# Turning Y into the FFN's input on VectorE, in 16 transposes of 32 rows, instead of on TensorE, from chunk 2 on

## The chip, the cores and the metric

One core of one Trainium2 chip. The metric is the device time of one execution in microseconds (us), on the slowest core, which here is the only one. Medians are over runs of one set; the ratio is the mean time of one kernel's fast runs over that of the other's of the same rounds, so it is not quite the ratio of the medians.

## The reference, cut to what matters

```python
def _attn_ref(q, k, v, beta):              # B=4, H=8, S=768, D=48
    k_n = k / (np.linalg.norm(k, axis=-1, keepdims=True) + 1e-06)
    for t in range(S):
        y[:, :, t] = einsum('bhd,bhde->bhe', q[:, :, t], state)
        v_old = einsum('bhde,bhd->bhe', state, k_n[:, :, t])
        state = state + beta[t] * outer(k_n[:, :, t], v[:, :, t] - v_old)
    return y

x = y.transpose(0, 2, 1, 3).reshape(B * S, H * D)      # (3072, 384)
out = (silu(x @ w_gate) * (x @ w_val)) @ w_out         # d_ff = 1536
```

The kernel walks through the sequence in 12 chunks of 64 positions. A chunk's Y comes out with the token on the partition (128 rows: two batches of 64 positions) and 768 columns. The FFN's products contract over the 384 features, so the FFN needs them on the partition: x_ffn, 128 partitions by 3 parts by 256 tokens. Turning Y into x_ffn is what the change is about.

## The kernel before

While TensorE does the FFN of chunk c, the recurrence of chunk c+1 is done in steps between its products. The order on each engine is that of the program's text. One step of the recurrence ends in Y, the next one turns it:

```python
    # advance(c), its last two steps
        p_of_u()
        y = work.tile([128, NB, NJ, 2, D], FP32, name="y", tag="r", bufs=2)
        for bp in each:
            nc.scalar.copy(y[:, bp, :, 0], p_y[:, 0, bp])
            for b in range(2):
                nc.scalar.copy(y[half_of(b), bp, :, 1], p_y[half_of(1 - b), 1, bp])
        yield

        y_f = y.rearrange("p bp j par d -> p bp (j par d)")
        xts[c] = ffn_pool.tile([128, KT, TOK], FP32, name="x_ffn")
        p_f = ps_pair("p_f", "py")[:, :, 0 : KT * 128]
        ...
        for bp in range(NB):
            for t in range(KT):
                nc.tensor.transpose(p_f[:, t, bp], y_f[:, bp, at], ident)   # 6 products
        for bp in each:
            nc.scalar.copy(x_v[:, :, bp], p_f[:, :, bp])                    # the copy
        yield
```

VectorE's work between the FFN's products: h_f (gate times value), sums of h_f, the adds of the fast output, the steps of an inverse (two instructions each, tmp and zb, handed out by `fill`), and the turning of k and q in whole, into kt and qt, which TensorE needs for the products of k with k and of q with k ("Gram products" here, p_g). The traces count two instructions for each call of an FFN product, so six calls show as x12; the transposes of Y on TensorE count one.

```python
            nc.vector.transpose(xt, blocks...)       # kt and qt, 128x1024 each, in front of their Gram products
    ...
    def gate_val(c, f, fill, within=None):           # six times a chunk
        ... 6 products p_gate; sil on ScalarE; fill(2); 6 products p_val
        nc.vector.tensor_tensor(out=hs[c, f], in0=sil, in1=ps["p_val"], op=ALU.mult)
        ... sums_of_h
        fill(3)
```

And in the fast output VectorE's adds stand between products. `product(1, 1)` is called twice with one tile, and between the two calls `add` reads it:

```python
        product(1, 0, ...); add(o[1][:, right], o[0][:, right], p[1, 0])
        fill(2)
        point(c + 1)                                 # the next chunk's step: here Y is turned, for even chunks
        product(0, 0, ...); nc.scalar.copy(o[0][:, left], p[0, 0])
        for f in range(0, FH, 2):
            minus(h_of(c, f + FH, 0), h_of(c, f + FH, 0), s_of(2, f))      # three
        product(1, 1, lambda f: s_of(1, f), ...)
        add(o[1][:, right], o[1][:, right], p[1, 1])
        point(c + 1)                                 # kt and qt
        product(1, 0, ...); add(o[1][:, left], o[0][:, right], p[1, 0])
        product(1, 1, lambda f: h_of(c, f + FH, 0), quarter(1, 1))         # same tile as above
```

Of the kernel before, what the change touches and what calls it, by code (L numbers as in the profile page):

```python
# [16 lines left out]
R = 32  # L17
# [4 lines left out]
def kernel(  # L22
# [25 lines left out]
    nc = tc.nc  # L48
# [4 lines left out]
    NB = B // 2  # L53
    DM = H * D
    DFF = moe_w_gate.shape[1]
    KT = DM // 128
# [13 lines left out]
    def ps_pair(name, tag):  # L70

        return psum.tile([128, 2, 512], FP32, name=name, tag=tag, bufs=1)
# [17 lines left out]
    def slot(c):  # L90
        return c if c < AHEAD else (c - AHEAD) % (AHEAD - 1)

    def freed_by_k(c):

        return c - AHEAD if c < 2 * AHEAD - 1 else c - AHEAD + 1
# [21 lines left out]
    def load_k(c, dmas=(nc.sync,)):  # L117
        for n in range(2 * NB):
            bp, b = divmod(n, 2)
            dmas[n % len(dmas)].dma_start(  # L120
                out=knp[slot(c)][64 * b : 64 * b + 64, bp, :, 0:D],
                in_=halves(k, c, bp, b).rearrange("h p d -> p h d"),
            )
# [37 lines left out]
    def load_v(c):  # L161
        vin[c] = work.tile([128, 2, NB, NJ, D], FP32, name="vin", bufs=2)
        for bp in range(NB):
            for b in range(2):
                src = halves(v, c, bp, b).rearrange("(j par) p d -> par p j d", par=2)
                for par in range(2):
                    s = 64 * (b ^ par)
                    nc.sync.dma_start(out=vin[c][s : s + 64, par, bp], in_=src[par])
# [161 lines left out]
    kt, qt, a_sb, a_of, p_sb, xts = {}, {}, {}, {}, {}, {}  # L330
# [3 lines left out]
    def half_of(x):  # L334
        return slice(64 * x, 64 * x + 64)

    def every():
        for bp in range(NB):
            for j in range(NJ):
                for n, (par, b) in enumerate(ORDER):  # L340
                    yield bp, j, par, b, bp == 0 and j == 0
# [56 lines left out]
    def scale_v(c):  # L398
        r = vin[c].rearrange("p par bp j d -> p (par bp j) d")
        n = n_t[c // 2][:, c % 2, :, None].to_broadcast([128, HH, D])  # L400
        nc.vector.tensor_tensor(out=r, in0=r, in1=n, op=ALU.mult)
# [171 lines left out]
    def recur(p, m=D):  # L573
        p = p[:, :, 0 : NB * NJ * m]
        return p.rearrange("p x (bp j d) -> p x bp j d", bp=NB, j=NJ)
# [154 lines left out]
    def advance(c):  # L730

        kn = knp[slot(c)]
        zt = ztp[c // 2 % ZB][:, c % 2]
        zt = zt.rearrange("p (par bp j) i -> p par bp j i", par=2, bp=NB)
        if c > 0:
            scale_v(c)
        r = vin.pop(c)
        p_y = recur(ps_pair("p_y", "py"))
        if c > 0:
            p_r = recur(ps_pair("p_r", "px"))  # L740
            for bp, j, par, b, first in every():
                nc.tensor.matmul(  # L742
                    p_r[half_of(b ^ par), par, bp, j],
                    kt[c][half_of(par), bp, j, b],
                    state[half_of(par), b, bp, j],
                    start=first,
                    stop=True,
                    skip_group_check=True,
                )
            for bp, j, par, b, first in every():  # L750
                nc.tensor.matmul(  # L751
                    p_y[half_of(b ^ par), par, bp, j],
                    qt[c][half_of(par), bp, j, b],
                    state[half_of(par), b, bp, j],
                    start=first,
                    stop=False,
                    skip_group_check=True,
                )
            nc.vector.tensor_tensor(out=r, in0=r, in1=p_r, op=ALU.subtract)  # L759
        yield  # L760
        p_u = recur(ps_pair("p_u", "px"))
        for bp, j, par, b, first in every():
            nc.tensor.matmul(  # L763
                p_u[half_of(b), par, bp, j],
                zt[half_of(b ^ par), par, bp, j],
                r[half_of(b ^ par), par, bp, j],
                start=first,
                stop=True,
                skip_group_check=True,
            )  # L770
        uu = work.tile([128, 2, NB, NJ, D], FP32, name="uu", tag="r", bufs=2)
        each = range(NB) if c == 0 else (slice(0, NB),)
        for bp in each:
            nc.scalar.copy(uu[:, :, bp], p_u[:, :, bp])
        if c + 2 < NCH:
            load_v(c + 2)
        yield
        pq = p_sb.pop(c)

        def p_of_u():  # L780
            for bp, j, par, b, first in every():
                nc.tensor.matmul(  # L782
                    p_y[half_of(b ^ par), par, bp, j],
                    pq[half_of(b), par, bp, j],
                    uu[half_of(b), par, bp, j],
                    start=(c == 0 and first),
                    stop=True,
                    skip_group_check=True,
                )

        def of_state():
            p_s = recur(ps_pair("p_s", "px"))
            for bp, j, par, b, first in every():
                nc.tensor.matmul(  # L794
                    p_s[half_of(par), b, bp, j],
                    kn[half_of(b), bp, 2 * j + par],
                    uu[half_of(b), par, bp, j],
                    start=first,
                    stop=True,
                    skip_group_check=True,  # L800
                )
            if c > 0:
                nc.vector.tensor_tensor(out=state, in0=state, in1=p_s, op=ALU.add)
            else:
                nc.scalar.copy(state, p_s)
            for later in range(AHEAD, NCH):
                if freed_by_k(later) == c:
                    load_k(later)

        if 0 < c < NCH - 1:  # L810
            of_state()
# [7 lines that stand above are left out]

        y_f = y.rearrange("p bp j par d -> p bp (j par d)")  # L820
        xts[c] = ffn_pool.tile([128, KT, TOK], FP32, name="x_ffn")
        p_f = ps_pair("p_f", "py")[:, :, 0 : KT * 128]
        p_f = p_f.rearrange("p bp (t n) -> p t bp n", t=KT)
        for bp in range(NB):
            for t in range(KT):
                at = slice(t * 128, (t + 1) * 128)
                nc.tensor.transpose(p_f[:, t, bp], y_f[:, bp, at], ident)
        x_v = xts[c].rearrange("p t (bp n) -> p t bp n", bp=NB)
        for bp in each:
            nc.scalar.copy(x_v[:, :, bp], p_f[:, :, bp])  # L830
        yield
        if c == 0:
            of_state()
            yield
# [256 lines left out]
    def point(c):  # L1091

        mine = c < NCH and steps("advance", c) < 4 and may_advance(c)
        if mine and steps("advance", c) > 0:
            step("advance", advance, c)
        elif not prep_step(c - 1) and mine:
            step("advance", advance, c)

    def finish(c):

        if c < NCH:
            while not may_advance(c):
                fill_some(1000)
                prep_step(c - 1)
            while steps("advance", c) < 4:
                step("advance", advance, c)
# [190 lines left out]
```

## Time and profile before

| | before |
|---|---|
| median of 4 runs | 738.61 us (738.02 to 739.34) |
| span of the profiled run | 737.5 us |
| TensorE, VectorE, ScalarE busy | 697.5, 473.1, 154.7 us |
| one set of six products, start to next start | 0.66 us |
| ScalarE's copy behind it | 0.80 us |
| places with a set from chunk 2 on | 10 |

The rows for the operations that go (60 of the 72 products and 10 of the 13 copies), as the view of one tile gives them (shortest, median and longest time of one in ns; first and last start in us). The 0.27 us of one product is not what it costs, as the products overlap:

```profile
L827 PE MATMUL p_f<-ident,y x72: 272/273/472, 61.6 to 664.4; 128*128 128x128 f32 x72
L830 ACT COPY x_ffn<-p_f x13: 480/799/801, 63.1 to 664.7; 128x768 f32<-128x768 f32 x11, 128x384 f32<-128x384 f32 x2
```

### The profile page before, as it was taken

Reading aid. Unit: us, or ns where it says so; the run is one execution under the profiler, and the core shown is the slowest. Engines: PE = TensorE matmul, PEld = TensorE weight load, DVE = VectorE, ACT = ScalarE, POOL = GpSimd, SP = SyncE. Lnnn points to the kernel's source line nnn. Section 1 sums busy time; section 2 is a strip of 40 time slices with the busy share of each in tenths; the row PEclk is TensorE's granted clock in tenths of the full one; section 3 lists DMA queues with packets and bytes.
Section 4 is the critical chain, followed back from the end, with each engine's and each line's share of the span. In section 5 each row is a group of like instructions: output and inputs, shape, how many; then the busy total and the mean of one; then the engine's idle time right before and its main releaser. Section 6 shows DMA issues by size and latency. Waiting matters only on the chain.

```text
span 737.5 us, 22478 instructions
## 1 busy us (share of the span) xinstructions
PE 697.5 (95%) x10132; PEld 604.7 (82%) x10132; DVE 473.1 (64%) x977; ACT 154.7 (21%) x287; POOL 66.9 (9%) x46
## 2 busy tenths in 40 slices
PE   4657899999999999999999999999999999999997
PEld 3546788866787788988988988988988988989987
DVE  5999988978498163678854678854578853313122
ACT  3455443302401112011012011012011012021010
POOL 7008100201200000030000030000030000000000
PEclk9556999999999999999999999999999999999999
DMA  6775444121231012331302231302210100100000
GB/s 141 164 227 166 124 108 129 36 41 24 56 45 24 22 24 45 43 67 15 53 3 45 36 70 20 53 3 39 46 29 12 32 3 3 23 3 0 22 1 21
DMA packets 130735, 37.18 MB, mean 50 GB/s; under 512 B 122864, under 2 KB 125936, under 8 KB 130640
## 3 DMA queue, kind: packets, MB, share of 16 engines
q1 hardware_dynamic: 127184, 34.01, 22.7%
q10 hardware_dynamic: 3072, 1.57, 1.0%
q8 instruction: 79, 1.29, 0.7%
q0 software_dynamic: 384, 0.17, 0.1%
q14 instruction: 16, 0.13, 0.1%
HBM read 31.01 MB, written 4.72 MB: 48 GB/s over the span
## 4 chain that ended last, share of the span: by engine, by line
PE 83%; DVE 14%; issue 1%; DMA 1%; ACT 0%; ACTq 0%; SPq 0%; DVEq 0%
PE p_gate L847 23%; PE p_val L847 23%; PE p_o L959 17%; PE p_o L876 6%; DVE tmp L510 3%; PE p_g L444 3%; DVE zb L516 3%; PE p_u L763 2%; PE p_r L742 1%; PE p_s L794 1%; PE p_y L782 1%; PE p_y L751 1%; DVE last_h L287 1%; PE p_t L432 1%; DVE h_f L862 1%
## 5 line engine op out<-in xcount | busy, mean ns | idle before, releaser
L847 PE MATMUL p_gate<-x_ffn,wg_sb 128*128 128x256 f32 x864 | 204.4, 387 | 1.5 <-ACT x_ffn L830 1.5
L847 PE MATMUL p_val<-x_ffn,wv_sb 128*128 128x256 f32 x864 | 198.5, 379 | 0.0
L847 PEld LDWEIGHTS p_val<-x_ffn,wv_sb 128*128 128x128 f32 x864 | 163.8, 190 | 22.3
L847 PEld LDWEIGHTS p_gate<-x_ffn,wg_sb 128*128 128x128 f32 x864 | 161.1, 191 | 24.2 <-ACT x_ffn L830 2.0
L862 DVE TENSOR_TENSOR h_f<-sil,p_val 128x512 f32<-128x512 f32 x71 | 48.6, 684 | 147.5 <-PE p_val L847 147.0
L856 ACT ACTIVATE sil<-p_gate 128x512 f32<-128x512 f32 x72 | 43.0, 598 | 276.9 <-PE p_gate L847 247.3
L655 POOL TENSOR_TENSOR n_b<-mb,half 128x32 f32<-128x32 f32 x5 | 43.0, 8607 | 408.6 <-DVE mb L480 368.2
L959 PE MATMUL p_o<-wo_sb,h_f 128*128 128x192 f32 x432 | 75.6, 328 | 0.1
L959 PEld LDWEIGHTS p_o<-wo_sb,h_f 128*128 128x128 f32 x432 | 70.3, 190 | 1.2 <-DVE o_sb L969 0.7
L510 DVE TENSOR_TENSOR tmp<-zb,mb 128x31 f32<-128x31 f32 (+15 forms) x186 | 63.3, 340 | 12.2 <-PE p_j L630 6.8
L516 DVE TENSOR_TENSOR zb<-zb,tmp 128x31 f32<-128x31 f32 (+15 forms) x186 | 63.7, 343 | 6.5 <-DVE tmp L510 0.2
L969 DVE TENSOR_TENSOR o_sb<-o_sb,p_o 128x192 f32<-128x192 f32 x45 | 15.8, 350 | 53.4 <-PE p_o L959 36.2
L876 PE MATMUL p_o<-wo_sb,h_f 128*128 128x384 f32 x136 | 45.7, 490 | 0.0
L876 PEld LDWEIGHTS p_o<-wo_sb,h_f 128*128 128x128 f32 x136 | 25.3, 190 | 16.5
L959 PE MATMUL p_o<-last_k,h_f 128*128 128x192 f32 x180 | 32.2, 326 | 0.0
L959 PEld LDWEIGHTS p_o<-last_k,h_f 128*128 128x128 f32 x180 | 29.7, 190 | 0.0
L917 DVE TENSOR_TENSOR h_f<-h_f,h_f 128x256 f32<-128x256 f32 x54 | 22.4, 424 | 8.0 <-PE p_o L959 7.1
L959 PE MATMUL p_o<-last_h,h_f 128*128 128x192 f32 x144 | 26.3, 326 | 0.0
L959 PEld LDWEIGHTS p_o<-last_h,h_f 128*128 128x128 f32 x144 | 23.9, 190 | 0.0
L254 ACT ACTIVATE last_h<-last_h,rebias 128x512 int32<-128x512 uint32 (+2 forms) x26 | 15.3, 616 | 30.5 <-DVE last_h L246 30.4
L763 PEld LDWEIGHTS p_u<-vin,zt 64*64 64x64 f32 x768 | 13.7, 141 | 6.9 <-issue 3.2
L763 PE MATMUL p_u<-vin,zt 64*64 64x48 f32 x768 | 15.7, 228 | 2.4 <-DVE vin L759 1.2
(180 smaller groups left out, 692.6 us busy)
## 6 DMA issues: line engine op xcount, KB each, us to landing
vin<-in_v_dram SPq DMA_DIRECT2D x96, 48.0 KB
kn<-in_k_dram SPq DMA_DIRECT2D x40, 96.0 KB
out_dram<-o_sb SPq DMA_DIRECT2D x36, 96.0 KB
zt<-in_moe_w_out_dram SPq DMA_DIRECT2D x6, 384.0 KB
staged<-in_moe_w_out_dram SPq DMA_DIRECT2D x6, 384.0 KB
qpad<-in_q_dram SPq DMA_DIRECT2D x36, 64.0 KB
wo_sb<-in_moe_w_gate_dram SPq DMA_DIRECT2D x4, 512.0 KB
wo_sb<-in_moe_w_val_dram SPq DMA_DIRECT2D x4, 512.0 KB
```

Of the source, the lines that this page charges most:

```text
L444: nc.tensor.matmul(p_v[par][half_of(b if of_q else b ^ par), bp, j], kt[c][half_of(par), bp, j, b], xt[half_of(par), bp, j, b],)
L510: nc.vector.tensor_tensor(out=t_v, in0=zb[:, 0 : j + 1, j : j + 1].to_broadcast([128, j + 1, m]), in1=mb[:, j : j + 1, j + 1 : R].to_broad ...
L516: nc.vector.tensor_tensor(out=zb[:, 0 : j + 1, j + 1 : R], in0=zb[:, 0 : j + 1, j + 1 : R], in1=t_v, op=ALU.add,)
L655: nc.gpsimd.tensor_tensor(out=n, in0=mb.rearrange("p j i -> p (j i)")[:, 0 : R * R : R + 1], in1=half, op=ALU.pow,)
L763: nc.tensor.matmul(p_u[half_of(b), par, bp, j], zt[half_of(b ^ par), par, bp, j], r[half_of(b ^ par), par, bp, j], start=first, stop=True, ...
L847: nc.tensor.matmul(ps[name][:, i], w_sb[:, t, (f + i) * 128 : (f + i + 1) * 128], xts[c][:, t], start=(t == 0), stop=(t == KT - 1),)
L856: nc.scalar.activation(sil, ps[name], ACTF.Silu)
L862: nc.vector.tensor_tensor(out=hs[c, f], in0=sil, in1=ps["p_val"], op=ALU.mult)
L876: nc.tensor.matmul(p_o, hs[c, f - f % 2][:, f % 2, bp * 128 : (bp + 1) * 128], wo_sb[:, f], start=(f == 0), stop=(f == FT - 1),)
L917: nc.vector.tensor_tensor(out=out, in0=a, in1=b, op=ALU.subtract)
L959: nc.tensor.matmul(p[x, part], a(f - f % 2)[:, f % 2], b(f), start=not begun and f == 0, stop=f == FH - 1, skip_group_check=True,)
L969: nc.vector.tensor_tensor(out=out, in0=a, in1=b, op=ALU.add)
```

## The change

TensorE is 95% busy and VectorE 64%, so the change takes the turning from TensorE (and ScalarE) and gives it to VectorE from chunk 2 on. The new transposes turn Y in blocks of 32x32. One instruction takes 32 rows of Y and the six blocks that belong to one quarter of x_ffn's partitions; four quarters of each make 16.

```diff
         xts[c] = ffn_pool.tile([128, KT, TOK], FP32, name="x_ffn")
+        if c > 1:
+            y_q = y_f.rearrange("p bp (t q d) -> p q t bp d", t=KT, q=4)
+            x_q = xts[c].rearrange("p t (bp q n) -> p q t bp n", bp=NB, q=4)
+            for of_x in range(4):
+                for of_y in range(4):
+                    nc.vector.transpose(
+                        x_q[R * of_x : R * of_x + R, of_y],
+                        y_q[R * of_y : R * of_y + R, of_x],
+                    )
+            yield
+            return
         p_f = ps_pair("p_f", "py")[:, :, 0 : KT * 128]
```

## The prediction

> **What bounds the kernel now.** I read the page first: busy shares, then the row of 40 slices, then the chain that ended last.
>
> ```profile
> span 737.5 us, 22478 instructions
> PE 697.5 (95%) x10132; PEld 604.7 (82%) x10132; DVE 473.1 (64%) x977; ACT 154.7 (21%) x287; POOL 66.9 (9%) x46
> PE   4657899999999999999999999999999999999997
> DVE  5999988978498163678854678854578853313122
> PE 83%; DVE 14%; issue 1%; DMA 1%; ACT 0%; ACTq 0%; SPq 0%; DVEq 0%
> ```
>
> From slice 6 on, TensorE is full and carries the chain; VectorE has 36% idle on average. That average invites the change: take work from the full engine, give it to the idle one. But VectorE's row swings between 3 and 8 with the period of two chunks, and the chain holds 14% DVE. The question is what VectorE does at the ten places where the new transposes stand. The program's order is fixed by hand, and comparing the instruction orders of the two kernels confirms it: nothing moves except that each set of six products leaves TensorE's order, each copy leaves ScalarE's, and each set of 16 transposes enters VectorE's.
>
> First, what TensorE gains. The timeline around one set (chunk 5's):
>
> ```profile
> 334.04 0.82 PE L827 MATMUL p_f<-ident,y 128*128 128x128 f32 x6
> 334.70 0.38 PE L847 MATMUL p_gate<-x_ffn,wg_sb 128*128 128x256 f32 x1
> ```
>
> Column one is the start, column two the time. The products are pipelined: the next product starts 0.66 us after the first of the six, not 0.82. So a set costs TensorE 0.66 us, and that is all that can be won in a place where TensorE is the bound.
>
> Second, where VectorE is the bound. The same chunk, ten microseconds later:
>
> ```profile
> 344.49 0.43 DVE L516 TENSOR_TENSOR zb<-zb,tmp 128x256 f32<-128x256 f32 x1
> 344.87 1.25 DVE L422 STREAM_TRANSPOSE kt<-qpad 128x1024 f32<-128x1024 f32 x1
> 346.04 1.20 DVE L422 STREAM_TRANSPOSE qt<-qpad 128x1024 f32<-128x1024 f32 x1
> 346.17 0.34 PE L444 MATMUL p_g<-kt 64*64 64x64 f32 x8 [0.94 <-DVE kt L422]
> ```
>
> TensorE already waits 0.94 us for VectorE's kt. The stretch from the h_f that starts at 334.31 (as TensorE ends p_val) to kt is full on VectorE; the stretches view gives it as follows (columns: stretch, length, busy of PE, PEld, DVE, ACT, POOL, clock):
>
> ```profile
> 334.30:344.90 10.60, 10.60 (x54) 9.33 (x51) 9.97 (x25) 1.99 (x3) 0.00 (x0) 1.00 0.00 0
> ```
>
> 9.97 of 10.60 us busy, the rest the 0.02 to 0.3 us between dependent instructions. There is no room in it, and the new transposes of chunk 5 stand in its middle, after the step that ends at 338.7. The timeline shows the same wait at 457.21 (0.95 us, chunk 7) and 568.36 (1.04 us, on qt, chunk 9).
>
> **What the Trainium skill says.** "VectorE: DVE Perf Modes", section "The three transpose paths": VectorE transposes only within 32x32 blocks, TensorE a full 128x128 into PSUM. Hence 16 instructions, one per pair of quarters. The trace has no 128x128 case on VectorE, but it has transposes of 32 rows into another quarter:
>
> ```profile
> 240.22 1.54 DVE L688 STREAM_TRANSPOSE z<-zt 32x256 f32<-32x256 f32 x4
> ```
>
> The same page, "Two Vector instructions with no wait between them": an instruction whose input starts in another quadrant than the last input is held until all earlier ones have finished. The trace agrees: these four start at 240.22, 240.59, 240.99, 241.36; 0.37 apart within a quadrant, 0.40 to 0.41 where the quadrant changes. All 16 new ones change the input quadrant each time.
>
> "TensorE: Matmul & The Clock Gate", section "Part 1: The HAM clock gate": after an idle window of about 3.4 us the array runs at half clock, until a busy window of that length. The trace agrees in its first 70 us (same columns; the clock is the number after POOL's):
>
> ```profile
> 29.80:33.20 3.40, 1.20 (x80) 1.06 (x72) 3.16 (x8) 1.07 (x2) 0.00 (x0) 1.00 0.52 94
> 33.20:63.90 30.70, 16.93 (x606) 14.23 (x597) 29.70 (x91) 19.23 (x51) 5.48 (x1) 0.50 0.65 174
> 63.90:67.30 3.40, 3.26 (x8) 2.64 (x9) 3.40 (x10) 1.43 (x3) 3.40 (x1) 0.50 0.81 201
> 67.30:70.70 3.40, 3.40 (x136) 2.87 (x135) 3.40 (x8) 1.82 (x3) 3.40 (x1) 1.00 0.54 176
> ```
>
> One window with 1.20 us of work of 3.40 dropped the clock to 0.5; it stayed there at half use and came back after one window with 3.26 of 3.40. So a wait of under 1 us costs itself, and a wait of 7 us costs something more.
>
> **The change part by part.** Removed: 10 sets of six products, 10 x 0.66 = 6.6 us of TensorE, and 10 ScalarE copies of 0.80 us (ScalarE is 21% busy: worth nothing by itself). Added: 160 transposes of 32x192. A column costs 1.07 ns (kt's 1024 columns take 1240 ns, z's 256 columns 415 ns in the mean). 64 columns fewer than z is 0.07 us less, so held ones follow each other at 0.405 - 0.07 = 0.335 us. A set takes T = 16 x 0.335 = 5.4 us, and 54 us for all ten; VectorE goes from 473 to about 527 us busy. I take the runs of 32 neighbouring columns at both ends, as z has them, for full speed. Now by place:
>
> Chunks 5, 7, 9 (transposes inside the full stretch): kt or qt comes T later, so the product that waits for it starts T later; 0.66 us saved on TensorE only lengthens the wait, to 0.94 + 0.66 + 5.4 = 7.0 us. Cost 5.4 each, 16.2 together. Nothing gives it back, as VectorE's next stretch starts again from a TensorE product.
>
> Chunk 2:
>
> ```profile
> 192.63 1.13 PE L847 MATMUL p_gate<-x_ffn,wg_sb 128*128 128x256 f32 x4 [0.52 <-ACT x_ffn L830]
> 193.04 0.28 DVE L516 TENSOR_TENSOR zb<-zb,tmp 128x112 f32<-128x112 f32 x1
> ```
>
> Here x_ffn is needed at once: TensorE waits for it 0.52 us even now. The new order puts the transposes behind the step that ends at 193.32, so x_ffn is whole at 193.35 + 5.4 = 198.75 and p_gate starts at about 198.8 instead of 192.63: cost 6.2.
>
> Chunks 4, 6, 8, 10 (transposes within the fast output of the chunk before):
>
> ```profile
> 297.15 0.35 DVE L969 TENSOR_TENSOR o_sb<-o_sb,p_o 128x192 f32<-128x192 f32 x1 [1.54 <-PE p_o L959]
> 298.46 0.43 DVE L917 TENSOR_TENSOR h_f<-h_f,h_f 128x256 f32<-128x256 f32 x1 [0.95 <-PE p_o L959]
> ```
>
> The transposes go between these two. They end at 297.5 + 5.4 = 302.9; the first h_f then ends at 303.35. TensorE needs it for the product that starts at 303.46 now and could start at 302.80 then. So the wait eats the 0.66 us, net about 0; kt and qt then follow at 305.4 and 306.6, which delays the qt product (306.48 now) by 0.2 in three of the four. Cost 0.6 together.
>
> Chunks 3 and 11: VectorE is idle behind the transposes (15.3 us before 257.07 in chunk 3; in chunk 11 no inverse is left to compute), and x_ffn is needed 10 and 24 us later. Gain 2 x 0.66 = 1.3.
>
> Sum: 6.2 + 16.2 + 0.6 - 1.3 = +21.7 us. To this comes the clock at the four long waits (chunks 2, 5, 7, 9: 6.7 to 7.0 us of idle TensorE, enough for a whole idle window). After each, TensorE runs at half clock for the rest of a window and then one whole one, 3.4 to 6.8 us, and loses half of that: an estimate of 2.2 us each from the lines above, 8.8 together. 738.3 + 21.7 + 8.8 = 768.8; I predict 768.
>
> **The rivals.** (a) TensorE stays the bound and all transposes hide: 738.3 - 6.6 and chunk 2's 0.5 to 1 us of waits gives 731, still within 2%. VectorE's 64% and the idle 36% speak for it; the full stretches before kt and the wait already there speak against it. (b) The waits come but the clock stays up: 760. The drop after a window with 1.20 us of work speaks against it. (c) The transposes run slower, as those with scattered columns do (32x1024 in 1941 to 2145 ns against 1216 for a plain one): a set would take about 8.6 us, each of eight places would pay 3.2 more, and the time would be near 794. The contiguous runs of 32 speak against it. (d) Transposes without holding, 0.30 apart, T = 4.8: eight places pay 0.6 less each, 764.
>
> **Range and chances.** T between 4.8 and 5.9 moves the sum by about 4 us each way, the clock's share lies between 4 and 14. I put the range at 756 to 781. 2% slower is 753, below even case (b). Faster by 2% is not reachable, as the whole TensorE cost removed is 0.9%. Chances: faster 0.01, within 2% 0.06, slower 0.93.
>
> **What would show it.** In the new profile: x_ffn transposes of 330 to 350 ns, sets of 5.2 to 5.6 us; TensorE waits of about 7 us for kt, kt and qt before the Gram products of three chunks and of over 6 us for x_ffn before chunk 2's first p_gate; a clock of 0.5 for a few us behind each; waits under 1 us in the four fast outputs; none in chunks 3 and 11. Wrong would be: sets much longer or shorter than 5.4, a TensorE row without holes, or a clock that stays at 1.0 behind them.

## The result, and the profile after

777.43 us (median of 4, 776.09 to 778.19) against 738.61 us: ratio 1.0523, 95% interval 1.0504 to 1.0542. The change makes the kernel 5% slower. The prediction was 768, with a range of 756 to 781.

The page of the changed kernel, its busy line, the rows by slices and the chain:

```profile
span 776.4 us, 22499 instructions
PE 702.4 (90%) x10072; PEld 608.2 (78%) x10072; DVE 530.5 (68%) x1137; ACT 146.5 (19%) x277; POOL 67.7 (9%) x46
PE   5657999998799999896999896999897899899997
DVE  5999989797498455879753969754778764626122
PEclk8657999999799999997999998999999899999999
PE 71%; DVE 24%; issue 2%; POOL 1%; DMA 1%; ACT 0%; SPq 0%; DVEq 0%
```

VectorE's share went up by only four points, and still 10% of the chain moved to it. TensorE's row, full from slice 6 on before, has holes, and the clock's row dips in four of those slices. TensorE is busy *longer* than before (702.4 against 697.5 us) although 60 products are gone: mostly work done at half clock (1.6 us of it lie in the first 150 us, where the two runs differ anyway).

The transposes themselves, in the view of the tile (times of one in ns):

```profile
L828 DVE STREAM_TRANSPOSE x_ffn<-y x160: 358/370/375, 193.2 to 711.3; 32x192 f32<-32x192 f32 x160
```

Chunk 5's turn in the timeline. Before, TensorE waited 0.94 us for this kt:

```profile
348.43 6.11 DVE L828 STREAM_TRANSPOSE x_ffn<-y 32x192 f32<-32x192 f32 x16
...
360.74 1.25 DVE L422 STREAM_TRANSPOSE kt<-qpad 128x1024 f32<-128x1024 f32 x1
...
362.04 1.98 PE L444 MATMUL p_g<-kt 64*64 64x64 f32 x64 [7.63 <-DVE kt L422]
```

The set takes 6.11 us, kt comes that much later, and the product behind kt waits 7.63 us. The product takes 1.98 us for what took 1.16. The stretches around it show why (columns: stretch, length, busy time of PE, PEld, DVE, ACT, POOL, clock):

```profile
356.60:366.90 10.30, 4.86 (x132) 4.74 (x133) 9.89 (x21) 0.60 (x1) 0.00 (x0) 0.50 0.20 27
366.90:370.30 3.40, 3.40 (x23) 3.40 (x22) 3.23 (x9) 0.32 (x1) 0.00 (x0) 1.00 0.66 85
```

The clock fell to 0.5 while TensorE waited and stayed there for almost 5 us after it had work again. In these traces it holds each value for 3.41 us or a whole multiple of that; one such stretch of 3.41 us is called a window below. Chunk 2, where x_ffn itself is late:

```profile
193.22 6.11 DVE L828 STREAM_TRANSPOSE x_ffn<-y 32x192 f32<-32x192 f32 x16
...
199.38 4.65 PE L859 MATMUL p_gate<-x_ffn,wg_sb 128*128 128x256 f32 x12 [7.30 <-DVE x_ffn L828]
```

And the fast output in front of chunk 4, where I had expected nothing worth naming:

```profile
305.64 6.11 DVE L828 STREAM_TRANSPOSE x_ffn<-y 32x192 f32<-32x192 f32 x16
...
311.78 1.09 DVE L929 TENSOR_TENSOR h_f<-h_f,h_f 128x256 f32<-128x256 f32 x3
312.80 0.35 DVE L981 TENSOR_TENSOR o_sb<-o_sb,p_o 128x192 f32<-128x192 f32 x1
...
313.20 2.22 PE L971 MATMUL p_o<-wo_sb,h_f 128*128 128x192 f32 x12 [2.01 <-DVE o_sb L981]
```

Where the 39 us went. I took the start of the first p_gate of every gate/value step in both traces and followed the shift between them; behind chunk 0, where it swings by up to 1.2 us and ends at -0.05, the shift changes only at the places of the change and just behind them. A long wait's own part is read at the start of the product that waits, the rest up to the next FFN step is put down to the clock.

| place | predicted | the wait, net | behind it, clock 0.5 | sum |
|---|---|---|---|---|
| chunk 2 | 6.2 | 6.80 | 1.79, and 0.34 at a Gram product for which VectorE is late | 8.93 |
| chunk 5 | 5.4 | 6.02 | 1.60 | 7.62 |
| chunk 7 | 5.4 | 6.02 | 1.18 | 7.20 |
| chunk 9 | 5.4 | 5.92 | 2.56 | 8.48 |
| chunks 4, 6, 8, 10 | 0.6 together | 1.63, 1.62, 1.62, 1.63 | 1.57 behind chunk 8's | 8.07 |
| chunks 3, 11 | -1.3 | -0.66, -0.65 | none | -1.31 |
| clock | 8.8 | | (8.70, in the rows above) | |
| all | 30.5 | | | 38.99 |

The spans differ by 776.4 - 737.5 = 38.9.

### The profile page after: what moved, and what is told of

Its sections match the earlier page's. It is cut to its first block, busy times and chain, and to the rows that moved or that the text cites. A ratio compares the mean times of both kernels' runs of the same rounds, so it can differ in the third digit from the quotient of the medians.

```text
span 776.4 us, 22499 instructions
## 1 busy us (share of the span) xinstructions
PE 702.4 (90%) x10072; PEld 608.2 (78%) x10072; DVE 530.5 (68%) x1137; ACT 146.5 (19%) x277; POOL 67.7 (9%) x46
## 3 DMA queue, kind: packets, MB, share of 16 engines
q10 hardware_dynamic: 3072, 1.57, 0.9%
## 4 chain that ended last, share of the span: by engine, by line
PE 71%; DVE 24%; issue 2%; POOL 1%; DMA 1%; ACT 0%; SPq 0%; DVEq 0%
PE p_gate L859 22%; PE p_val L859 21%; PE p_o L971 14%; DVE x_ffn L828 6%; DVE tmp L510 4%; DVE zb L516 4%; PE p_g L444 3%; PE p_o L888 2%; PE p_u L763 1%; PE p_s L794 1%; PE p_r L742 1%; PE p_y L782 1%; PE p_y L751 1%; DVE h_f L929 1%; POOL n_b L655 1%
## 5 line engine op out<-in xcount | busy, mean ns | idle before, releaser
L859 PE MATMUL p_gate<-x_ffn,wg_sb 128*128 128x256 f32 x864 | 208.1, 392 | 8.2 <-DVE x_ffn L828 7.3
L859 PEld LDWEIGHTS p_gate<-x_ffn,wg_sb 128*128 128x128 f32 x864 | 164.0, 194 | 32.3 <-DVE x_ffn L828 7.4
L971 PE MATMUL p_o<-wo_sb,h_f 128*128 128x192 f32 x432 | 79.1, 338 | 8.1 <-DVE o_sb L981 8.1
L971 PEld LDWEIGHTS p_o<-wo_sb,h_f 128*128 128x128 f32 x432 | 73.5, 197 | 9.9 <-DVE o_sb L981 9.2
L828 DVE STREAM_TRANSPOSE x_ffn<-y 32x192 f32<-32x192 f32 x160 | 59.1, 369 | 2.0
L888 PEld LDWEIGHTS p_o<-wo_sb,h_f 128*128 128x128 f32 x136 | 25.4, 190 | 16.7
L444 PE MATMUL p_g<-kt 64*64 64x64 f32 x576 | 13.2, 257 | 15.4 <-DVE kt L422 15.4
L444 PEld LDWEIGHTS p_g<-kt 64*64 64x64 f32 x576 | 12.0, 169 | 18.2 <-DVE kt L422 16.6
```

Of the source, the lines that this page charges most:

```text
L444: nc.tensor.matmul(p_v[par][half_of(b if of_q else b ^ par), bp, j], kt[c][half_of(par), bp, j, b], xt[half_of(par), bp, j, b],)
L828: nc.vector.transpose(x_q[R * of_x : R * of_x + R, of_y], y_q[R * of_y : R * of_y + R, of_x],)
L859: nc.tensor.matmul(ps[name][:, i], w_sb[:, t, (f + i) * 128 : (f + i + 1) * 128], xts[c][:, t], start=(t == 0), stop=(t == KT - 1),)
L888: nc.tensor.matmul(p_o, hs[c, f - f % 2][:, f % 2, bp * 128 : (bp + 1) * 128], wo_sb[:, f], start=(f == 0), stop=(f == FT - 1),)
L971: nc.tensor.matmul(p[x, part], a(f - f % 2)[:, f % 2], b(f), start=not begun and f == 0, stop=f == FH - 1, skip_group_check=True,)
```

## The experiments

My theory after the result: what a set costs is decided by what stands behind it in VectorE's queue. Where TensorE soon needs something from that queue (kt or qt, the adds of the fast output, x_ffn itself in chunk 2), the set's 6.1 us, less what room there is, goes on the path; a wait of this length drops TensorE's clock on top. Where nothing is needed, the set is free and 0.66 us are won. Rivals: the transposes cost wherever they stand; it is the amount of VectorE's work and not its place; x_ffn's own arrival is what is late; the low clock is only a sign of waiting and costs nothing of its own.

"Before" ran at 738.6 to 739.1 us (medians).

### Chunks 3 and 11 alone

```diff
-        if c > 1:
+        if c in (3, 11):
```

> The transposes on VectorE in chunks 3 and 11 alone, where VectorE was idle. My theory (a set pays 0.66 us wherever VectorE has room, and costs where it has none): 738.6 - 2 x 0.66 = 737.3 us, no new wait of TensorE. Rival (the transposes slow TensorE wherever they stand, by what they share with it): at or above 738.6.

Measured: 737.50 us (5 runs), ratio 0.9980, interval 0.9967 to 0.9993. The set in chunk 3 takes the same 6.11 us and is hidden whole. So the transposes cost TensorE nothing by themselves: 0.66 us is won each time, as predicted, and the first rival falls.

### Chunks 4, 6, 8, 10 alone

```diff
-        if c > 1:
+        if c in (4, 6, 8, 10):
```

> Chunks 4, 6, 8 and 10 alone, placed as in the change. My theory, by the trace of the change: four waits of about 2.0 us in the fast outputs, net 1.62 each, so 738.6 + 6.5 = 745 us, plus up to 1.6 for each drop of the clock that such a wait sets off. Rival (the prediction's sum, in which these four are worth 0.6 together): 739.2.

Measured: 748.12 us (4 runs), ratio 1.0122. The four waits are there, 2.01 us each. The time is 3 us above my sum; in the profiled run two of the waits dropped the clock, and each of these cost 1.6 us more than the others. One p_gate started 1.15 us late for no reason that the profile names; it was seen in one look only, in a run 1.2 us over the median. The stretches around the second wait (columns as above):

```profile
415.90:419.30 3.40, 1.39 (x9) 1.18 (x8) 3.34 (x9) 0.00 (x0) 0.00 (x0) 1.00 0.00 0
419.30:422.70 3.40, 3.40 (x64) 2.96 (x65) 1.64 (x3) 0.00 (x0) 0.00 (x0) 0.50 0.48 60
422.80:426.20 3.40, 3.40 (x89) 3.07 (x80) 3.13 (x5) 0.00 (x0) 0.00 (x0) 1.00 0.66 89
```

1.39 us of work in a window of 3.4 was too little, and the next window ran at half clock. The waits in front of chunks 4 and 8 were just as long and dropped nothing: it depends on how the wait lies to the windows. All 20 waits of this length in the traces of five kernels (the change, this one, both with unread products and the one with neighbouring columns, all below) bear this out: the nine that left one window with 1.40 to 1.44 us of work dropped the clock, the eleven that left 1.67 us or more in each did not.

### The same four, one step earlier

```diff
                 nc.scalar.copy(y[half_of(b), bp, :, 1], p_y[half_of(1 - b), 1, bp])
-        yield
+        if c not in (4, 6, 8, 10):
+            yield
 ...
-        if c > 1:
+        if c in (4, 6, 8, 10):
 ...
             yield
+            if c % 2 == 0:
+                yield              # the number of steps stays
             return
```

> The same four chunks, but with the transposes one step of the recurrence earlier, right behind the copies of Y, so that VectorE does them in the 5 us in which it was idle before the adds of the fast output. My theory: the waits go and the 0.66 us stay as a gain: 738.6 - 2.6 = 736.0 us. Rival (the cost is in the amount of VectorE's work, not in its place): 745 as with the later place.

Measured: 736.07 us (5 runs), ratio 0.9962, interval 0.9950 to 0.9975. Same instructions, same amount of VectorE work, only moved ahead of two adds: from 748.1 to 736.1 us. The timeline in front of chunk 4:

```profile
291.30 6.12 DVE L829 STREAM_TRANSPOSE x_ffn<-y 32x192 f32<-32x192 f32 x16 [0.17 <-ACT y L817]
...
297.45 0.80 DVE L984 TENSOR_TENSOR o_sb<-o_sb,p_o 128x192 f32<-128x192 f32 x2
298.17 1.09 DVE L932 TENSOR_TENSOR h_f<-h_f,h_f 128x256 f32<-128x256 f32 x3
300.22 0.35 DVE L984 TENSOR_TENSOR o_sb<-o_sb,p_o 128x192 f32<-128x192 f32 x1 [0.96 <-PE p_o L974]
...
301.97 2.11 PE L974 MATMUL p_o<-wo_sb,h_f 128*128 128x192 f32 x12
```

The set fills time in which VectorE only waited, the two adds come late but nobody waits for them yet, and when the third add is due VectorE waits for TensorE again. The last product starts without a wait. It is the place, not the amount.

### Chunks 5, 7, 9 alone, and chunk 2 alone

```diff
-        if c > 1:
+        if c in (5, 7, 9):        # the other kernel: (2,)
```

> Chunks 5, 7 and 9 alone, placed as in the change. My theory: three waits of 7.6 us for kt, kt and qt; each delays the chain by 6.0 us and drops the clock for about 1.2 to 2.6 us of loss: 738.6 + 18 + 5 = 762 us. If the clock plays no part: 757.

> Chunk 2 alone. My theory: one wait of 7.3 us for x_ffn, 6.8 us later start of its first p_gate, and about 2 us at half clock: 747.4 us. If the clock plays no part: 745.4.

Measured: 762.88 us (ratio 1.0321) and 747.69 us (ratio 1.0118), 4 runs each. Both as expected with the clock's part, and above the figures without it. In the first profile the waits are 7.62 to 7.63 us and the clock is at 0.5 for 6.8, 10.2 and 10.2 us around them. Added up, the four partial kernels differ from before by -1.1 + 9.5 + 24.1 + 8.9 = 41.4 us, the change by 38.8: nearly additive. In the profiled runs one 2 us wait more dropped the clock than in the change, which makes 1.6 of the 2.6 us between them; the rest was not traced.

### The transposes into a tile that nobody reads

```diff
+            spare_x = work.tile([128, KT, TOK], FP32, name="spare_x", tag="r", bufs=2)
-            x_q = xts[c].rearrange("p t (bp q n) -> p q t bp n", bp=NB, q=4)
+            x_q = spare_x.rearrange("p t (bp q n) -> p q t bp n", bp=NB, q=4)
 ...
-            yield
-            return                 # TensorE's six products and the copy follow in all chunks
```

> TensorE's products and the copy are kept in all chunks, and the transposes run beside them into a tile that nobody reads. My theory (what costs is VectorE's time ahead of kt, qt and the adds, and only in chunk 2 the arrival of x_ffn itself): chunk 2's 8.9 us go, the rest stays, chunks 3 and 11 lose their 1.3 us gain: 777.4 - 8.9 + 1.3 = 769.8 us. Rival (it is x_ffn that comes late everywhere): 738.6.

Measured: 767.82 us (4 runs), ratio 1.0396. x_ffn is made on TensorE as before, at its old time, and yet nearly everything of the loss but chunk 2's is there. TensorE's wait for kt:

```profile
353.26 1.03 PE L444 MATMUL p_g<-kt 64*64 64x64 f32 x28 [6.96 <-DVE kt L422]
```

6.96 us instead of 7.63, the 0.66 us being TensorE's own products again; in the fast outputs 1.36 instead of 2.01. So outside chunk 2 the late thing is not x_ffn but what queues behind it. My figure was 2 us too high; no 2.0 us wait is left here that could drop the clock, and none dropped.

### TensorE kept at work while it waits: a miss, and again

```diff
         p_g = banks("p_g", tag or ("py" if of_q else "px"))
+        if (c, of_q) in WARM:      # first run: (6, False), (8, False), (10, True)
+            for n in range(15):    # again:     (8, False), (10, False), (10, True)
+                nc.tensor.matmul(p_g[n % 2][:, 0:256], wg_sb[:, 0, 0:128], wv_sb[:, 0, 0:256])
```

The real Gram products overwrite what these leave.

> The change, with 15 products of 128x256 that nobody reads put in front of the Gram products that wait for kt, kt and qt in chunks 5, 7 and 9: 6.5 us of work in waits of 7.6 us. My theory (the idle time drops the clock, the dropped clock costs 1.6 + 1.2 + 2.6 us behind these three waits): the waits stay, the clock stays at 1.0 behind them: 777.4 - 5.4 = 772 us. Rival (the low clock is no cost of its own): 777.4 or more.

Measured: 783.78 us (4 runs), ratio 1.0599: a miss, by an error of mine. I had taken the wrong Gram product for chunk 5's. One set of 15 landed in chunk 2, where nothing waits, and cost 6.3 us; chunk 7's wait stayed uncovered at 7.63 us with a low clock behind it. The two covered waits already showed the effect: the low clock behind them was gone. So I ran it with the right three:

> The earlier run of this kind had its first 15 unread products in front of a Gram product of chunk 2 that waits for nothing, where they cost 6.3 us, and left chunk 7's wait uncovered. Here they stand in front of the three that wait. My theory: idle stretches of 1.15 us instead of 7.6 in front of kt, kt and qt, no low clock behind them, and 777.4 - 1.6 - 1.2 - 2.6 = 772 us; the 2.0 us waits of the fast outputs may still drop the clock by up to 1.6 us each, in a different number of them. Rival (the low clock costs nothing of its own): 777.

Measured: 773.81 us (4 runs, 772.64 to 777.36), ratio 1.0488. In front of chunk 5's Gram product now:

```profile
353.16 6.64 PE L445 MATMUL p_g<-wv_sb,wg_sb 128*128 128x256 f32 x30
360.95 0.75 PE L450 MATMUL p_g<-kt 64*64 64x64 f32 x36 [1.15 <-DVE kt L423]
```

The stretch behind it (columns as above):

```profile
361.00:364.40 3.40, 3.40 (x135) 3.23 (x136) 3.26 (x7) 0.00 (x0) 0.00 (x0) 1.00 0.39 53
```

The product starts no earlier relative to what is before it, but the clock stays at 1.0 behind all three. Chunks 5, 7 and 9 now shift the rest by 6.05, 6.02 and 5.94 us, where the change had 7.62, 7.20 and 8.48: 5.3 us less by useless products alone. The whole times would not carry this, as their intervals overlap (1.0459 to 1.0517 here, 1.0504 to 1.0542 for the change); the places do. Five covered waits in the two traces cost 5.94 to 6.05 us; seven uncovered ones (three in the change, three with chunks 5, 7 and 9 alone, one in the first run here) 7.2 to 8.7. The low clock is a cost of its own. The median is 1.8 us above my figure; in the profiled run two of the fast outputs' waits dropped the clock, in the change's one. Single runs of one kernel spread by almost 5 us here, which is what one to three such drops more would make; that this is the cause of the spread was not looked at run by run.

### Why one transpose takes longer than I scaled

Two kernels with a wrong result:

```diff
# neighbouring columns instead of six runs of 32
-    x_q[R * of_x : R * of_x + R, of_y],  y_q[R * of_y : R * of_y + R, of_x]
+    x_q[R * of_x : R * of_x + R, 192 * of_y : 192 * of_y + 192],
+    y_q[R * of_y : R * of_y + R, 192 * of_x : 192 * of_x + 192]     # x_q, y_q: flat columns here
# each reads the quarter that it writes
-    y_q[R * of_y : R * of_y + R, of_x]
+    y_q[R * of_x : R * of_x + R, of_y]
```

> Wrong result on purpose: the 16 transposes take 192 neighbouring columns of Y and write 192 neighbouring columns of x_ffn, instead of six runs of 32. If the runs are what makes one take 0.369 us and not the 0.335 that I scaled from z's: 0.335 each, sets of 5.5 us, 8 places x 0.6 = 5 us less, 772 us. If the size of an instruction's fixed part was misjudged: 0.369 each and 777.

> Wrong result on purpose: each transpose reads the quarter that it writes, so that the quarters change only at every fourth one. If the change of the quarter holds an instruction until the one before has ended: three of four follow at about 0.31 us instead of 0.382, sets of 5.3 us, and 8 x 0.8 = 6 us less, 771 us. If not: 0.382 apart still, 777.

Measured: 777.24 us (ratio 1.0516) with neighbouring columns, as slow as the change: the runs of 32 cost nothing. With the quarters kept: 764.77 us (ratio 1.0349), 12.7 us less than the change and twice the 6 us that I had expected, as three of four follow at 0.26 to 0.30 us and not at 0.31. Its transposes in the view of the tile and in chunk 2's timeline:

```profile
L828 DVE STREAM_TRANSPOSE x_ffn<-y x160: 323/327/375, 193.0 to 695.5; 32x192 f32<-32x192 f32 x160
193.00 4.63 DVE L828 STREAM_TRANSPOSE x_ffn<-y 32x192 f32<-32x192 f32 x16
```

16 in 4.63 us instead of 6.11. Read one by one, those that stay within a quarter start 0.26 us behind the one before (0.30 behind one that changed it), those that change it 0.34; in the change, where all 16 change it, they start 0.382 apart. So a held instruction (one that waits until the one before has ended) starts 0.382 behind a held one, and 0.34 behind one that was not held. I had taken the second figure, from z's four, in which only every other one changes its quarter. A set is 1.48 us shorter, which at the eight places where it is on the path makes 11.8 us; the waits in the fast outputs shrink from 2.01 to 0.54 us and none of them drops the clock.

This order can't be had with a right result: each of the 16 pairs of quarters is needed once, so each instruction changes one quarter at least. An order in which most instructions change only the quarter that they write (the two loops swapped) was not run; every held instruction measured here changed the quarter that it reads.

### What beats both

Chunks 3 and 11 as in the change, 4, 6, 8 and 10 one step earlier, TensorE's products in 2, 5, 7 and 9:

```diff
-        yield
+        if c not in (4, 6, 8, 10):
+            yield
 ...
-        if c > 1:
+        if c in (3, 4, 6, 8, 10, 11):
```

> Both together: chunks 3 and 11 as in the change, 4, 6, 8 and 10 early, and TensorE's products kept in chunks 2, 5, 7 and 9. My theory: the gains add, 738.6 - 6 x 0.66 = 734.7 us. Rival (they don't add because some other wait ends the chain): 736 to 738.

Measured: 734.94 us (5 runs, 734.00 to 735.68), ratio 0.9946, interval 0.9934 to 0.9959. Correct, and 3.7 us faster than before. The shift between its trace and that of before falls by 0.66, 0.66, 0.66, 0.66, 0.66 and 0.65 us at the six chunks: the gains add.

## Why the prediction was right, point by point

- **TensorE's gain of 0.66 us a set: right.** 0.66 and 0.65 in chunks 3 and 11, and in all six places of the best version.
- **Chunks 5, 7, 9: the wait was right, its size 0.6 us too small.** Predicted 5.4 each and waits of 7.0; measured 6.0 and 7.6. The term is T: predicted 5.4, measured 6.11 (outside the 5.2 to 5.6 of its signs), because 0.335 us apart was read from a held instruction behind one that was not held. Held ones in a row are 0.382 apart.
- **Chunk 2: right**, 6.80 us against 6.2, the difference again T. The 0.34 us at a later Gram product was not foreseen.
- **Chunks 4, 6, 8, 10: this step failed.** The prediction let "the first h_f" end at 303.35 in time for the product, "net about 0", and expected waits under 1 us. In its place came waits of 2.01 us, net 1.6 each. 0.7 of it is T. About 1.0 is an instruction that I left out: the product goes on in the PSUM tile that the add in front of kt reads, so it starts behind the third h_f and that add, 1.45 us after the set's end and not 0.45. This was in the program's text and in the order of instructions, though not in the trace of before, where the add was done 1.4 us before the product.
- **The clock: right**, 8.8 us predicted, 8.70 measured. The agreement is a little better than earned: the four foreseen drops cost 7.13, and 1.57 came from a fifth in a fast output, where none was foreseen. One reading was loose: the window with 1.20 us of work was shown as agreeing with a rule about idle windows, and it was not idle; the drops at waits of only 2.0 us show the same. That the low clock is a cost of its own is shown by the runs with the unread products.
- **Chunks 3 and 11: right.** Nothing waits.
- **The rivals.** (a), all hidden, fell by the waits; the unread transposes show that VectorE's queue is the cause. (b), no clock loss, fell by the rows at 0.5. (c), slow scattered columns, fell by the run with neighbouring columns. (d), transposes that are not held, was measured at T = 4.63, by the kernel that keeps the quarters: 764.8 us against the 764 that the prediction gave for it (so close partly by chance, as T was smaller still and the fast outputs dearer than that sum had them).

The sum was 8.5 us short: 5.9 in the fast outputs, 2.7 at the other four long waits (T, and the 0.34 us), less 0.1 in the clock. The range held.

## What to carry to other kernels

An engine with a third of its time idle may still have no room where the new work lands; read the queue between the place and the next thing that another engine needs from it, to the last instruction, also those whose result was not waited for before. A wait of TensorE costs its length and, from about 2 us on in these runs, may cost another 1.2 to 2.6 us through the clock; the waits of 1.36 us dropped nothing. A move that loses as a whole can win in parts: six of the ten places were free here, four of them after moving the work ahead of two instructions.

## What the Trainium skill lacked or had wrong

- "VectorE: DVE Perf Modes", section "Two Vector instructions with no wait between them", says which instructions are held and gives no time for it. In these runs 32x192 transposes start 0.382 us apart when each is held, 0.34 when a held one follows one that was not, and when not held 0.26 (0.30 behind a held one); a set of 16 takes 6.11 us against 4.63.
- The same page, section "The three transpose paths", compares one 128x128 transpose of two-byte elements on each engine and gives no time for fp32 or for 32 rows that go to another quarter. Here one 32x192 takes 0.37 us on VectorE, the whole 128x768 takes 16 of them and 6.11 us, and TensorE's six products cost 0.66 us of its time and a copy of 0.80 us on ScalarE.
- "TensorE: Matmul & The Clock Gate", section "Part 1: The HAM clock gate", gives an idle window as what throttles the array. In these runs a window need not be idle: 1.39 us of work in 3.4 us dropped the clock, after a wait of only 2.0 us, and where each window kept 1.67 us or more it did not drop at a wait of that length. Its window length agrees: the low stretches lasted 3.4, 6.8 or 10.2 us.
